# A two-batch conformer block on one core: the second batch's first query group is scored by quads, LayerNorm statistics beside attention move to ACT

## The chip, the cores and the metric

The kernel runs on one core of one Trainium2 chip. The metric is the device time of one execution in microseconds (us); the median of three runs is given, and beside it the time of the one execution that was profiled. All tensors in memory are bf16.

## The reference

Two sequences of T = 4000 tokens with D = 512 channels go through one conformer block. F is 2048; every LayerNorm is without weights.

```python
h = _layernorm(x);  x1 = x + 0.5 * (_silu(h @ w_ff1_a) @ w_ff1_b)
h = _layernorm(x1); q, k, v = h @ w_q, h @ w_k, h @ w_v
p = _softmax(einsum('btd,bsd->bts', q, k) * D ** -0.5)
x2 = x1 + einsum('bts,bsd->btd', p, v) @ w_o
h = _layernorm(x2) @ w_pw1
h = h[..., :D] * _sigmoid(h[..., D:])
dc = depthwise convolution of h over time, 3 taps per channel
dc = (dc - mean) / sqrt(var + 1e-5)      # per channel, over both sequences
x3 = x2 + _silu(dc) @ w_pw2
h = _layernorm(x3); x4 = x3 + 0.5 * (_silu(h @ w_ff2_a) @ w_ff2_b)
return _layernorm(x4)
```

## The kernel before

**Stages.** The tokens of a sequence are cut into seven chunks of 512 and one of 416, so there are 16 chunks for the two sequences. First the feed-forward block runs over all chunks, writes each chunk's residual to DRAM, and writes the normalised tokens ("keys") to DRAM as `keysd`. Then comes attention, with one query group per chunk: groups 0 to 7 are the first sequence, 8 to 15 the second. The convolution's first matmuls and taps of earlier groups run in the same slots. After attention come the end of the convolution and the second feed-forward block.

**Attention.** w_q and w_k are folded into one matrix M, w_v and w_o into another, so that keys and values are both the normalised tokens. A query group has 32 slots `kt`, one per tile of 128 keys; the last tile is a tail of 32. In a *plain* group each key tile is scored by four matmuls that stream 512 query columns. In a *quad* group tiles 0, 1 and 30 are scored plainly and the other 28 in seven quads of four tiles: `score_quad` makes a 2x2 product by seven products instead of eight (the form of Strassen and Winograd). Each of the seven is four matmuls of 256 columns. ACT copies the first and the fifth product, DVE adds them to others on the way (tiles `s`, `xt` in the trace, by their memories), and ACT takes the exponents. A quad needs three sums of key tiles (`k_sums`, stored to DRAM as `kfd`, fetched by `k_stream`), one difference that is put over a key tile, and sums of the queries (`q_sums`). In the kernel before, groups 0 and 8 are plain (`plain = g % TCB == 0`), and make the key sums of their sequence while they run. The product of the exponents with the values is by seven products in all groups; its sums on DVE are `pair_sums`, which also adds up the softmax's denominators. The second sequence's value sums are made ahead, in groups 1 to 5, by `v_ahead`: load, four DVE sums, stores.

**What happens around a group.** `keys_swap` replaces the first sequence's keys by the second's in groups 7 and 8: `key_queries` issues one DMA transpose for each of the 32 key tiles. `units_late` ends the group before: its last value products, `sums_by_query` (the denominators turned by DMA transposes and reduced by one DVE instruction), and `project` in slots 9 and 13, whose `residual` on DVE adds the attention to the tokens. Then `ln_job` makes LayerNorm's statistics (BATCH_NORM_STATS2 and BATCH_NORM_AGGREGATE on DVE, a power on POOL), and normalises on ACT. `tail_scores`, for the 32 last keys, comes in slot 21.

**Who sets the order.** The program is written down once as nodes with their reads and writes, and then `Plan` orders it for each engine by costs and due times (`n.late`): it is a list scheduler, with DMA on SP's queue. An engine executes its own list in order, with waits on semaphores. The costs that matter here are

```python
if e == "ACT":
    return 170 + 0.83 * n + (200 if isinstance(call.kw.get("scale"), bass.AP) else 0)
```

so an instruction on ACT has no extra cost for bringing out an accumulated sum. Every instruction of the kernel is issued by one helper, so all rows of the profile have the line L93, and tiles tell them apart.

Of the kernel before, what the change touches and what calls it, by code (L numbers as in the profile page):

```python
# [109 lines left out]
class Plan:  # L110
# [161 lines left out]
    def once(self):  # L272

        pe, T = self.pe, self.T
        for n in reversed(self.nodes):
            if n.e != "PE":
                n.late = min([s.late - self.lag(n, s) - (self.SPARE if n.size else 0) for s in n.succs] + [pe[min(n.at, len(pe) - 1)].late + 40000])
# [273 lines left out]
class Conformer:  # L551
# [35 lines left out]
    def memory(self):  # L587
# [119 lines left out]
        self.b_kfd = [[Buf("kfd") for _ in range(QUADS)] for _ in range(B)]  # L707
        self.vhd = nc.dram_tensor("vhd", [PAIRS, 128, 2 * D], BF16, kind="Internal").ap()
# [150 lines left out]

        self.hl = C.view(oHL, 1024).rearrange("p (h c k) -> p h c k", h=2, c=DC)  # L860
# [3 lines left out]
        self.b_sq = [Buf("sq") for _ in range(2)]  # L864
# [237 lines left out]

    def ln_job(self, c, kind, eng="DVE", plan=(1, 1, 2, 2, 3, 4, 5, 5, 6, 6), slot=None, pe=None):
# [122 lines left out]
    def residual(self, ps, b_ps, g, scalar, b_scalar=(), rows=slice(0, TILE)):  # L1226

        self.S.op("DVE", lambda e: e.scalar_tensor_tensor(
            out=self.XT[g][rows], in0=ps[rows], scalar=scalar, in1=self.XT[g][rows], op0=ALU.mult, op1=ALU.add),
            reads=[b_ps, self.bx[g]] + list(b_scalar), writes=[self.bx[g]])  # L1230
# [367 lines left out]
    def q_group(self, b, qc, dc):  # L1598
# [5 lines left out]
        for cc in range(DC):  # L1604
            self.mm(ps[:, 0:W], self.M[:, cc, dc * 128:(dc + 1) * 128], lin[:, cc, lo:lo + W],
                    cc == 0, cc == DC - 1, [self.b_M] + self.b_lnT[sl], b_ps)
        self.act(self.qT[s][:, dc, 0:W], ps[:, 0:W], AF.Copy, [b_ps], [self.b_qT[s][dc]])
# [148 lines left out]
    def pair_sums(self, g, j, step):  # L1756
# [20 lines left out]
        if step == 6:  # L1777
            S.op("DVE", lambda e: e.tensor_tensor(out=acc[:, 0], in0=acc[:, 0], in1=acc[:, 1], op=ALU.add),
                 reads=[self.b_acc[s]], writes=[self.b_acc[s]])
            return  # L1780
        sig = [ft[:, 0:2, at + k, 0:hw] for k in range(n)]
        if j == 0:
            S.op("DVE", lambda e: e.tensor_copy(acc, sig[0]), reads=b_f[0:2], writes=[self.b_acc[s]])
        elif j == GROUPS - 1:
            S.op("DVE", lambda e: e.tensor_tensor(out=acc, in0=acc, in1=sig[step - 4], op=ALU.add),
                 reads=b_f[0:2] + [self.b_acc[s]], writes=[self.b_acc[s]])
        else:
            two = self.P30[:, 0:W].rearrange("p (h k) -> p h k", h=2)
            out, x, y, rd, b_out = ((two, sig[0], sig[1], b_f[0:2], self.b_P30), (acc, acc, two, [self.b_P30, self.b_acc[s]], self.b_acc[s]))[step - 4]
            S.op("DVE", lambda e: e.tensor_tensor(out=out, in0=x, in1=y, op=ALU.add), reads=rd, writes=[b_out])  # L1790
# [115 lines left out]

    def v_back(self, j, which):
# [37 lines left out]
    def k_stream(self, g, q):  # L1945
        n, b = (QUADS * g + q) % 2, g // TCB
        self.load(self.KF[n].rearrange("p m u j k -> p (m u j k)"), self.kfd[b][q], self.b_KF[n], reads=[self.b_kfd[b][q]])
# [56 lines left out]
    ASIDE = {3: (5, 7), 4: (5, 7), 5: (5, 7), 6: (5, 7), 16: (0,), 20: (0,), 21: (1,)}  # L2004
# [35 lines left out]
    def forms(self, g, kt):  # L2040

        plain, more = g % TCB == 0, g + 1 < NCK and (g + 1) % TCB
# [11 lines left out]
        else:  # L2054
# [3 lines left out]
            if kt == 1 and g % TCB == 1:  # L2058
# [39 lines left out]
    def units_late(self, o, kt):  # L2098
# [5 lines left out]
        elif kt < 7:  # L2104
# [7 lines left out]
            if kt == 3 and o == NCK - 2:  # L2112
                self.sums_direct(o % TCB % 2)
        for ti in {9: (0, 1), 13: (2, 3)}.get(kt, ()):
            self.project(o, ti)
# [856 lines left out]
```

## Time and profile before

| | |
|---|---|
| median of 3 runs | 1879.53 us (1877.93 to 1880.09) |
| the profiled execution | 1879.47 us |
| its span, first to last instruction | 1875.6 us, mean granted TensorE clock 0.998 |
| busy: PE / DVE / ACT / POOL | 1857.5 / 1548.0 / 1278.0 / 124.2 us |
| DMA, mean over the span | 123 GB/s |

In the rows, PE is the matmul engine, PEld its weight loads, DVE the vector engine, ACT the scalar engine, POOL GpSimd, and SP the queue that issues the DMAs. A row names what is written and read as out<-in by the memories of the program: `s` and `y` are the PSUM banks, `keys` holds the key tiles, `xt` the residual tokens and the sums for the quads, `sums` the exponents and their sums, `work` the queries, transposed tokens and LayerNorm's small values, `wff` in attention the convolution's buffers and the staging for sums made ahead. The span's stages are feed-forward to about 403 us, attention from there to about 1400, the turn to the second feed-forward block until about 1450, and that block to the end. Group 8 lies at about 892 to 958 us.

### The profile page before, as it was taken

The numbers are of one execution on the slowest core, as the hardware profiler recorded it, in microseconds if no ns is written. First come the engines' busy times: TensorE is split into PE (matmuls) and PEld (weight loads), VectorE is DVE, ScalarE is ACT, GpSimd is POOL, SyncE is SP. The second block draws the span as 40 slices with busy tenths as digits, with TensorE's granted clock in tenths as the row PEclk, the third lists the DMA queues.
The fourth block names the chain that finished last, engine by engine and source line by source line (L and its number), as shares of the span: only waits on it lengthen the run. The fifth ranks groups of instructions, "written<-read, shape, count | busy, mean of one in ns | idle before, by whom it ended". The sixth has DMA issues, their size and how long they took to land.

```text
span 1875.6 us, 38994 instructions
## 1 busy us (share of the span) xinstructions
PE 1857.5 (99%) x15384; PEld 1445.4 (77%) x15384; DVE 1548.0 (83%) x3293; ACT 1278.0 (68%) x2190; POOL 124.2 (7%) x241
## 2 busy tenths in 40 slices
PE   9999999999999999999999999999999999999998
PEld 5888888866777777777677777777764888888886
DVE  7789989868778888877878788778878889889885
ACT  5777777754556666666557666666657787777774
POOL 1000000000000000000000001000011000000010
PEclk9999999999999999999999999999999999999999
DMA  7333344197545555448954444444365222221211
GB/s 197 86 89 91 80 112 107 53 275 208 172 142 159 155 171 160 117 130 175 254 123 133 134 119 114 126 138 122 107 205 158 66 69 69 72 54 48 63 33 56
DMA packets 325013, 231.51 MB, mean 123 GB/s; under 512 B 204179, under 2 KB 295638, under 8 KB 324566
## 3 DMA queue, kind: packets, MB, share of 16 engines
q1 hardware_dynamic: 324294, 228.68, 44.2%
q8 instruction: 123, 2.02, 0.4%
q14 instruction: 68, 0.56, 0.1%
q10 hardware_dynamic: 528, 0.26, 0.0%
HBM read 128.44 MB, written 55.79 MB: 98 GB/s over the span
## 4 chain that ended last, share of the span: by engine, by line
PE 97%; DVE 1%; ACT 1%; DMA 0%; issue 0%; SPq 0%; DVEq 0%; ACTq 0%
PE s L93 49%; PE y L93 49%; DVE work L93 1%; ACT work L93 0%; DVE wff L93 0%; DMA xt<-in_x_dram 0%; ACT sums L93 0%; DVE xt L93 0%; DVE s L93 0%; ACT xt L93 0%; ACT s L93 0%; DVE sums L93 0%; DVE keys L93 0%; ACT keys L93 0%; SPq L93 0%
## 5 line engine op out<-in xcount | busy, mean ns | idle before, releaser
L93 ACT ACTIVATE sums<-s 128x512 bf16<-128x512 f32 (+2 forms) x494 | 289.1, 587 | 234.3 <-PE s L93 232.8
L93 ACT ACTIVATE keys<-s 128x512 bf16<-128x512 f32 (+2 forms) x284 | 165.2, 587 | 141.4 <-PE s L93 115.8
L93 DVE TENSOR_TENSOR sums<-sums 128x512 bf16<-128x512 bf16 (+3 forms) x528 | 201.8, 399 | 63.5 <-ACT sums L93 53.1
L93 PE MATMUL y<-work,keys 128*128 128x256 bf16 x1920 | 244.8, 273 | 0.0
L93 PE MATMUL s<-work,keys 128*128 128x256 bf16 (+5 forms) x1456 | 225.1, 292 | 0.8 <-ACT sums L93 0.6
L93 PE MATMUL y<-wff,keys 128*128 128x256 bf16 (+3 forms) x1592 | 209.2, 276 | 0.1
L93 DVE BATCH_NORM_STATS2 work<-xt 128x6 f32<-128x512 bf16 x311 | 205.6, 683 | 3.9 <-DMA xt<-in_x_dram 3.3
L93 PEld LDWEIGHTS y<-work,keys 128*128 128x128 bf16 x1920 | 187.9, 98 | 25.1
L93 PE MATMUL y<-sums,keys 128*128 128x256 bf16 (+1 forms) x1440 | 204.8, 270 | 0.0
L93 PE MATMUL s<-sums 128*128 128x256 bf16 x1296 | 194.5, 273 | 0.0
L93 DVE TENSOR_TENSOR keys<-keys 128x1024 bf16<-128x1024 bf16 (+2 forms) x262 | 170.2, 663 | 26.2 <-ACT keys L93 20.8
L93 PE MATMUL y<-work,wff 128*128 128x256 bf16 (+2 forms) x1116 | 184.0, 292 | 0.0
L93 PEld LDWEIGHTS y<-wff,keys 128*128 128x128 bf16 (+1 forms) x1592 | 151.2, 98 | 32.4 <-issue 3.3
L93 ACT ACTIVATE work<-xt,work 128x512 bf16<-128x512 bf16 x208 | 160.1, 805 | 10.9 <-DVE work L93 9.1
L93 POOL TENSOR_TENSOR work<-work 128x4 f32<-128x4 f32 (+3 forms) x92 | 88.3, 963 | 1108.3 <-DVE work L93 1108.3
L93 PEld LDWEIGHTS y<-sums,keys 128*128 128x128 bf16 x1440 | 139.1, 98 | 22.7 <-issue 0.2
L93 PEld LDWEIGHTS s<-work,keys 128*128 128x128 bf16 (+1 forms) x1456 | 119.3, 97 | 48.2 <-issue 4.7
L93 PEld LDWEIGHTS s<-sums 128*128 128x128 bf16 x1296 | 126.7, 98 | 20.0
L93 PE MATMUL s<-work,wff 128*128 128x512 bf16 (+5 forms) x668 | 140.5, 345 | 1.4 <-ACT work L93 1.1
L93 PE MATMUL y<-sums,xt 128*128 128x256 bf16 (+1 forms) x960 | 141.2, 270 | 0.3 <-DVE sums L93 0.3
L93 PE MATMUL s<-work 128*128 128x512 bf16 (+4 forms) x565 | 137.5, 373 | 2.4 <-DVE work L93 1.7
L93 PEld LDWEIGHTS y<-work,wff 128*128 128x128 bf16 x1116 | 108.2, 98 | 29.7
(140 smaller groups left out, 3195.8 us busy)
## 6 DMA issues: line engine op xcount, KB each, us to landing
xt<-kfd SPq DMA_DIRECT2D x98, 384.0 KB, 3.2
xt<-v12d SPq DMA_DIRECT2D x105, 256.0 KB, 3.0
xd<-xt SPq DMA_DIRECT2D x28, 512.0 KB, 3.0
xt<-xd SPq DMA_DIRECT2D x28, 512.0 KB, 3.8
out_dram<-xt SPq DMA_DIRECT2D x14, 512.0 KB, 2.9
xt<-in_x_dram SPq DMA_DIRECT2D x13, 512.0 KB, 4.1
dcvd<-wff SPq DMA_DIRECT2D x48, 128.0 KB, 2.7
keys<-dcvd SPq DMA_DIRECT2D x12, 512.0 KB, 4.0
```

The source lines that it names most:

```text
L93: return getattr(eng, self.name)(*self.args, **self.kw)
```

## The change

1. Group 8 scores by quads (`plain = g == 0`). The second sequence's key sums are made in groups 1 to 6 by `k_ahead`, in turn with `v_ahead`, which moves from a period of 10 slots to one of 6 for both: two DMA transposes of key tiles into a staging tile, four DVE sums, a store of the tiles to the new `khd`, and two stores to `kfd`. `k_back` brings the tiles back by a plain load of two tiles; only tiles 0, 1, 30 and the tail are still transposed in groups 7 and 8.
2. LayerNorm beside attention (`ln_beside`): the residual's DVE instruction also gives each token's sum, POOL scales it to a negative mean, ACT squares the centred tokens with an accumulated sum, and POOL does the rest. This takes the place of 4 statistics and 4 aggregates on DVE per group.
3. The denominators are reduced by four ACT copies with an accumulated sum per group, in place of one DVE reduction.
4. `pair_sums` adds the first two and the last pairs in bf16 before they go to the f32 sum.
5. `tail_scores` moves to slot 9 from group 1 on, always in bank 1; `touch` adds a matmul of 96 columns behind a 416-wide query projection that lands in bank 1.
6. In `Plan`, no instruction outside PE is due more than 8000 ns before PE's place in the program where it was written.

In whole numbers of instructions, from the built programs: PE has 112 fewer matmuls of 512 columns, 196 more of 256 and 4 more of 96; DVE has 119 instructions fewer, ACT 130 more, POOL 60 more, and SP issues 56 DMAs more.

```diff
-                n.late = min([s.late - ... for s in n.succs] + [pe[...].late + 40000])
+                n.late = max(pe[min(n.at, len(pe) - 1)].late - 8000, min([s.late - ... for s in n.succs] + [pe[...].late + 40000]))
...
+    def touch(self, ps, b_ps, W):
+        if W < CHUNK and b_ps is self.bank(1)[1]:
+            x = self.hT[0][:, 0, 0, :]
+            self.mm(ps[:, W:CHUNK], x, x[:, 0:CHUNK - W], False, True, [self.b_hT[0][0]], b_ps, skip_group_check=True)
...
+    def ln_spread(self, c, sl, ti):
+        x, b_x = self.tokens(c, ti)
+        self.act(self.ltm[ti][0:TILE, :], x, AF.Square, [b_x, self.b_mv[sl][ti]], [self.b_ltm[ti], self.b_st[sl][ti]],
+                 bias=self.mv[sl][:, ti, 0:1], accum_out=self.st[sl][:, ti, 1:2])
...
-        if j == 0:
-            S.op("DVE", lambda e: e.tensor_copy(acc, sig[0]), reads=b_f[0:2], writes=[self.b_acc[s]])
-        elif j == GROUPS - 1:
-            S.op("DVE", lambda e: e.tensor_tensor(out=acc, in0=acc, in1=sig[step - 4], op=ALU.add),
-                 reads=b_f[0:2] + [self.b_acc[s]], writes=[self.b_acc[s]])
+        t, b_t = (self.P30, self.b_P30) if j < GROUPS - 1 else (self.last7, self.b_last7)
+        if step == 4:
+            out, x, y, rd, wr = two, sig[0], sig[1], b_f[0:2], [b_t]
+        elif j == 1:
+            out, x, y, rd, wr = acc, two, f0[:, 0:2, 1, 0:hw], [b_t] + b_0[0:2], [self.b_acc[s]]
...
+    def k_ahead(self, i, step):
+        S, (q, u) = self.S, divmod(i, 2)
+        if step == 0:
+            for r in range(2):
+                src, rd = self.key_source(1, self.quad_tiles(q)[2 * u + r])
+                self.transpose(self.vst[:, r * D:(r + 1) * D].rearrange("p (c k) -> p c k", c=DC), src, rd, b_x)
+            return
+        if step < 5:
+            ...
+            S.op("DVE", lambda e: e.tensor_tensor(out=out, in0=x, in1=y, op=op), reads=rd + b_x, writes=wr)
+            return
+        self.store(self.khd[i], self.vst, b_x, [self.b_khd[i]])
+        self.store(form[:, 0:2, u], ..., b_2, [self.b_kfd2[q][2 * u]])
+        self.store(form[:, 2, u], self.vs1, b_1, [self.b_kfd2[q][2 * u + 1]])
+
+    def k_back(self, i):
+        self.load(self.hq[:, q, u].rearrange("p r e j k -> p (r e j k)"), self.khd[i], b, reads=[self.b_khd[i]])
...
-            W, plain = width(g), g % TCB == 0
+            W, plain = width(g), g == 0
...
+                if kt == (9 if g else 21):
+                    self.tail_scores(g)
...
-                if kt == 21:
-                    self.tail_scores(g)
...
+            if ti % 2:
+                self.ln_middle(self.ln_conv, slice(ti - 1, ti + 1))
...
-        i, r = divmod(at - KT - 4, 10)
-        if 0 <= i < PAIRS:
-            for n in {0: (0,), 4: (1, 2), 5: (3, 4), 8: (5,)}.get(r, ()):
-                self.v_ahead(i, n)
+        i, r = divmod(at - KT - 4, 6)
+        for n in {0: (0,), 2: (1, 2), 3: (3, 4), 5: (5,)}[r] if r in (0, 2, 3, 5) else ():
+            if i % 2 == 0 and 0 <= i // 2 < PAIRS:
+                self.v_ahead(i // 2, n)
+            elif i % 2 and 0 <= i // 2 < 2 * QUADS:
+                self.k_ahead(i // 2, n)
...
-                    self.key_queries(1, k)
+                    if k < 2 or k > KT - 3:
+                        self.key_queries(1, k)
+                    elif k % 2:
+                        self.k_back((k - 2) // 2)
...
-            S.op("DVE", lambda e: e.tensor_reduce(
-                self.sq[s], self.sT[0:TILE].rearrange("p h c k -> p c h k"), AX.XY, ALU.add),
-                reads=self.b_sT, writes=[self.b_sq[s]])
+            for ti in range(TPC if not self.any_score else 0):
+                x = self.sT[0:TILE, :, ti]
+                self.act(x, x, AF.Copy, self.b_sT, [self.b_sqs[s][ti]], accum_out=self.sq[s][:, ti:ti + 1])
...
-                self.ln_job(g - 1, "in", "ACT", (1, 2, 5, 6, 7, 8, 8, 9, 10, 11), slot=0)
+                self.ln_beside(g - 1, self.ln_conv, (2, 3, 6, 7, 7, 8, 9, 10, 11))
```

More of the change, by code (lines that the diff above doesn't have):

```diff
@@ L1946, in k_stream @@
         n, b = (QUADS * g + q) % 2, g // TCB
[L1947 removed]
+        self.load(self.KF[n].rearrange("p m u j k -> p (m u j k)"), self.kfd[b][q], self.b_KF[n],
+                  reads=self.b_kfd2[q] if b else [self.b_kfd[b][q]])
     def score_quad(self, g, q, step):
@@ L2040, in forms @@
     def forms(self, g, kt):
-        plain, more = g % TCB == 0, g + 1 < NCK and (g + 1) % TCB
+        plain, more = g == 0, g + 1 < NCK
         if more and 27 <= kt < 31:
```

85 lines of the change are left out of this document (67 added, 18 removed).

## The prediction, made before the changed kernel was run

> **What bounds the kernel now.** I read the page first (busy shares and the chain), then busy time by stage, then PE's own waits in those stages, then ACT's and PE's single rows. The page:
>
> ```profile
> PE 1857.5 (99%) x15384; PEld 1445.4 (77%) x15384; DVE 1548.0 (83%) x3293; ACT 1278.0 (68%) x2190; POOL 124.2 (7%) x241
> ...
> PE 97%; DVE 1%; ACT 1%; DMA 0%; issue 0%; SPq 0%; DVEq 0%; ACTq 0%
> ```
>
> The chain that ended last is PE for 97% of the span, at a mean granted clock of 0.998. Time comes out only where PE has fewer columns to stream or waits less. The table by stage has a window, its length, then busy us and counts of PE, PEld, DVE, ACT, POOL, then clock, DMA share, GB/s. The windows are query group 8 (the second batch's first, plain before), steady quad group 10, and group 15 (416 queries):
>
> ```profile
> 892.00:958.00 66.00, 65.14 (x455) 39.92 (x453) 52.03 (x126) 35.68 (x61) 2.94 (x11) 1.00 0.84 224
> 1020.00:1083.00 63.00, 63.00 (x517) 47.70 (x515) 48.41 (x102) 38.31 (x68) 2.78 (x7) 1.00 0.44 122
> 1334.00:1387.00 53.00, 51.05 (x498) 41.93 (x496) 42.24 (x98) 35.53 (x69) 2.73 (x9) 1.00 0.52 162
> ```
>
> A steady quad group keeps PE busy without a hole while DVE works 48 and ACT 38 of 63 us. Group 8 is longer, has holes, and has the highest DMA share of the three (0.84). PE's waits (who waited for whom: us, times, longest), for 835 to 958 us and then for 1334 to 1403 us:
>
> ```profile
> PE s L93 <- ACT sums L93: 0.6, 1, 0.6
> PE s L93 <- DVE s L93: 0.4, 1, 0.4
> PE s L93 <- DVE sums L93: 0.3, 1, 0.3
> PE s L93 <- DVE xt L93: 0.2, 1, 0.2
> ```
>
> ```profile
> PE s L93 <- ACT sums L93: 0.7, 2, 0.6
> PE s L93 <- DVE s L93: 0.4, 1, 0.4
> PE s L93 <- DVE xt L93: 0.4, 1, 0.4
> PE y L93 <- DVE sums L93: 0.3, 1, 0.3
> ```
>
> The same view for 958 to 1334 us, groups 9 to 14, is empty. For group 1 (460 to 521) it has 0.6 us in two waits. So the query groups hold 1.5 + 1.8 + 0.6 = 3.9 us of PE idle in 11 waits. What PE does per matmul comes from its timeline (start, length, count), once for 512 columns and once for 256:
>
> ```profile
> 26.25 2.75 PE L93 MATMUL s<-work,wff 128*128 128x512 bf16 x12
> 28.84 0.60 PE L93 MATMUL y<-work,keys 128*128 128x256 bf16 x4
> ...
> 489.20 0.60 PE L93 MATMUL y<-sums,xt 128*128 128x256 bf16 x4
> 489.63 0.60 PE L93 MATMUL s<-xt 128*128 128x256 bf16 x4
> 490.07 0.60 PE L93 MATMUL s<-work,keys 128*128 128x256 bf16 x4
> 490.51 0.60 PE L93 MATMUL y<-sums,xt 128*128 128x256 bf16 x4
> ```
>
> Start to start, 512 columns cost 2.59/12 = 0.216 us and 256 columns (490.51 - 489.20)/12 = 0.109 us. A 256-wide record lasts 0.273 us, so its shown end runs 0.164 us into its successor: each wait costs about 0.16 us more than its shown idle. The 11 waits cost 3.9 + 1.8 = 5.7 us.
>
> **The change, part by part.**
>
> *Quads in group 8.* 28 key tiles of 4 matmuls of 512 columns go: 112 x 0.216 = 24.2 us. Seven quads of 7 products of 4 matmuls of 256 come: 196 x 0.109 = 21.4 us. That is **-2.8 us** on the path. The rows bear this out directly, because groups 9 to 14 run this same mix without a hole. [...]
>
> *Four filler matmuls (touch)* of 96 columns after the 416-wide query projections: rows have 56 ns for 128 columns and 98 ns for a weight load, so 0.2 to 0.4 us; I take **+0.2**, nearest to the matmul row.
>
> *Group 8's own waits* (0.6 + 0.3 us in 892 to 958, with the overlap 1.2 us) sit in the plain scoring's exponents. In the quad form that follows, the view is empty. **-1.2 us**; bounds 0 and -1.2.
>
> *Work taken from DVE.* Per group it loses 4 statistics (0.686), 4 aggregates (0.185), one reduction over the transposed sums (1.215), the shift (0.165), a copy (0.42), and trades one f32 add (0.685) for a bf16 one (0.42): 5.5 of about 48 us. The tail scores leave slot 21, about where groups 1, 7 and 15 wait, for slot 9. The remaining waits there cost 5.7 - 1.2 = 4.5 us; seven of the nine were ended by DVE. Bounds 0 and -4.5; I take half, **-2.2 us**, as ACT ended the other two and gets more work.
>
> *Work given to ACT.* Per group 4 squares of 512 (0.60) and 4 copies of 256 (between 0.29 at 128 and 0.60 at 512, taken as 0.39), each with an accumulator read:
>
> ```profile
> 35.99 1.23 ACT L93 ACTIVATE work<-s 128x512 bf16<-128x512 f32 x2 [1.14 <-PE s L93]
> 37.11 0.19 ACT L93 ACTIVATION_READ_ACCUMULATOR work<-s 128x1 f32 x1
> 37.20 0.59 ACT L93 ACTIVATE keys<-s 128x512 bf16<-128x512 f32 x1
> ```
>
> That is 4 x 0.79 + 4 x 0.58 = 5.5 us shown, on 38 to 42 of 63. It lies beside PE, but ACT's queue is in order: behind a square stand exponents and the copy of the first product, for which PE's next product waits. The planner's cost for an activation (170 + 0.83n) has no term for the read, and the read puts off the next start by 0.09 us, so ACT runs late against its order by 8 x 0.09 = 0.74 us per group if nothing absorbs it. What absorbs it (ACT's groups in 958 to 1335 us; last field: idle before, and who ended it):
>
> ```profile
> L93 ACT ACTIVATE sums<-s 128x512 bf16<-128x512 f32 x136 | 80.9, 595 | 80.2 <-PE s L93 79.5
> ...
> L93 ACT ACTIVATE xt<-s 128x512 f32<-128x512 f32 x42 | 25.1, 597 | 25.6 <-PE s L93 25.3
> ```
>
> ACT sits idle 0.6 us on average before an exponent and before the first product's copy, so nearly all is absorbed. Bounds 0 and 15 x 0.74 = +11.1 us; I take **+1.0**, near the covered end. Without that cover it would be the whole 11.1. DVE's four residual sums per group also bring out an accumulator; no row has that on DVE, and with ACT's read (0.09) as a stand-in it is 0.4 us per group against 5.5 taken off: nothing.
>
> *Key sums ahead.* Groups 1 to 6 get 14 sets: two transposes, four DVE sums (0.28 each), three stores. Group 8 loses 28 sums of 0.42, its own 7 stores and 28 of the transposes in this row:
>
> ```profile
> L93 SPq DMA_TRANSPOSE keys<-keysd x30: 1188/1202/1863, 835.5 to 929.1; - x30
> ```
>
> SP's queue takes 28 x 1.2 + 42 x 0.45 = 53 us more over some 370 us; behind them stand the streams of key and value sums, issued about five slots (10 us) before use, that land in 3.2 us, so nothing waits. The DMA share there (0.55) has room; group 8's 0.84 falls, and its 14 plain loads (5.2 to 5.4 us for 256 to 512 KB in the loads of values) are issued 5 to 24 slots (10 us or more) ahead. A wait is added: the first sum waits for transposes (3.5 us to land) at the head of DVE's queue, with pair sums and the adds that PE needs behind it. DVE waited like this for transposes up to 0.9 us in groups 1, 2 and 11, and PE's only waits in these groups come 28 us later. I price it at 0, bounds 0 and 14 x 0.9 = +12.6 us.
>
> *New order elsewhere.* The limit on due times (8000 ns) moves ACT and DVE instructions in the feed-forward stages too, though PE's first 3,604 matmuls keep their order. No PE wait shows between 50 and 400 or 1450 and 1850 us. The tail between (1403 to 1450) has chained waits that can fall either way: 0, within 1.5.
>
> Sum: -2.8 + 0.2 - 1.2 - 2.2 + 1.0 = **-5.0 us**. The profiled execution took 1879.47 us (span 1875.6 and 3.9 around it), the median is 1879.53, so the forecast is **1874.5 us**.
>
> **Rivals.** 0.2% is 3.8 us, about what a measurement of this kernel can tell from no change.
> - *All waits of the query groups go*, DVE being what ended most: -2.8 + 0.2 - 5.7 = -8.3, 1871.2. For: DVE ended seven of those nine. Against: group 15 packs the same instructions into 53 us.
> - *Only the columns count*: the waits come back as others, as ACT takes up what DVE gives: -2.6, 1876.9. For: three of the eleven waits are ACT's already.
> - *ACT becomes late (the slower side)*: the reads and 5.5 us more per group delay the first product's copy. All 0.74 us exposed in 15 groups gives -6.0 + 11.1 = +5.1, 1884.6. It is slower by 3.8 us from 9.8 us, 0.65 per group, on. Against: 0.6 us idle before that copy.
> - *Late transposes hold DVE*, all 14 exposed: -5.0 + 12.6, 1887.
> - *Weight loads show*: if the 84 extra loads (98 ns) did not hide behind 256-wide matmuls, +8.2 - 2.8 and the other terms (-2.2) make +3.2, 1882.7, within 0.2%. The 0.109 us row, with one load to each matmul, excludes it. [...]
>
> **How the numbers follow.** Forecast 0.46; all waits go 0.16; columns only 0.23; ACT late 0.10; transposes 0.04; weight loads 0.01. Faster by over 0.2% is the first two, 0.62; same is columns only and the weight loads, 0.24; slower the other two, 0.14. Range 1869.5 to 1882: the low end is all waits and 1.5 from the tail; the high end reaches into the late cases and leaves some 0.1 beyond.
>
> **What would show it.** Right: 112 fewer matmuls of 512 columns and 196 more of 256; group 8 some 4 us shorter with an empty PE wait view; transposes gone from 835 to 930 us; fewer waits in groups 1, 7, 15. Wrong: PE waits on ACT in groups 9 to 14, where there are none now, DVE waits on wff<-keysd transposes followed by PE holes, or a new hole in the feed-forward stages.

## The result, and the profile after

After takes 1895.71 us in the median (1893.55 to 1898.54, 4 runs), before 1879.07 beside it (1877.93 to 1880.09, 4 runs): a ratio of 1.0087, 95% interval 1.0071 to 1.0103. The change costs 16.6 us where 5 us of gain were forecast. The profiled execution of after took 1898.54 us, its span is 1894.0, 18.4 us longer than before's. First the page's busy line and chain:

```profile
PE 1865.9 (99%) x15472; PEld 1451.1 (77%) x15472; DVE 1471.5 (78%) x3234; ACT 1316.3 (69%) x2436; POOL 132.9 (7%) x301
...
PE 87%; DMA 5%; DVE 4%; ACT 3%; issue 1%; SPq 0%; POOL 0%; DVEq 0%; ACTq 0%
```

PE is still 99% busy, but the chain that ended last is PE for 87% only, where before it was 97%. DMA, which was 0% of the chain, is 5%, and DVE 4%. DVE's own work fell by 76 us (1548.0 to 1471.5) and ACT's rose by 38, as the change says: more room on DVE, and a later end.

Where the time went can be read from one kind of PE's rows, the last value product of each group (`y<-wff,keys 32*128`), which comes early in the next group. Its first start in each group marks the same place in every kernel. Before has it at 460.95 us for group 0, at 892.80 for group 7, at 958.28 for group 8 and at 1387.32 for group 15; after at 460.74, 906.13, 970.08 and 1403.22. So groups 1 to 7 are 13.5 us longer, group 8 is 1.5 us shorter, groups 9 to 15 are 4.1 us longer, and what lies around them 2.3. The loss sits where the key sums are made ahead, not where ACT alone has more work.

Group 8 and the steady group 10, in windows that follow these marks (length, then busy us and counts of PE, PEld, DVE, ACT and POOL, clock, DMA share, GB/s):

```profile
906.00:970.00 64.00, 62.41 (x535) 46.94 (x532) 45.22 (x103) 44.94 (x89) 3.81 (x15) 1.00 0.83 220
1034.10:1097.10 63.00, 63.00 (x514) 47.40 (x514) 43.29 (x96) 42.79 (x86) 3.27 (x11) 1.00 0.43 121
```

Group 10 is as long as it was and PE has no hole in it, with DVE down from 48.4 to 43.3 us and ACT up from 38.3 to 42.8. Group 8 has the 455 matmuls of before turned into 535, and holes of 1.6 us. PE's waits (the lines of 0.8 us or more in all), first for groups 1 to 6 (460 to 849), then for groups 7 and 8 (849 to 970):

```profile
PE s L93 <- DVE s L93: 3.7, 6, 2.1
PE s L93 <- DVE xt L93: 2.1, 4, 1.0
PE s L93 <- ACT s L93: 0.8, 1, 0.8
```

```profile
PE s L93 <- ACT s L93: 1.7, 2, 1.3
PE s L93 <- DVE s L93: 1.0, 3, 0.4
```

In groups 1 to 6, where before had 0.6 us in two waits (460 to 835), PE waits 6.6 us on the first three lines, and DVE is what it waits for nearly always. What DVE and ACT themselves wait for over the whole span is new:

```profile
DVE sums L93 <- DMA work<-work: 15.3, 15, 4.2
DVE wff L93 <- DMA wff<-keysd: 13.1, 13, 2.6
ACT work L93 <- DMA work<-work: 9.5, 9, 2.7
```

Before, DVE's line for `wff<-keysd` was 0.5 us in one wait, its line for `sums` behind `work<-work` 5.6 in eleven, and ACT had none. The three lines belong to different stages. The thirteen waits on `wff<-keysd` all lie in groups 1 to 6: ten (10.4 us) end with a transpose for the key sums, three (2.7 us) with a load for the value sums, which go through the same staging tile. ACT's nine waits lie in attention too, behind the transposes that turn the softmax's denominators; before, DVE stood 2.2 us in three waits for these. DVE's fifteen waits of `sums` on `work<-work` lie outside attention, before 308 us and after 1467 us, in the two feed-forward blocks. SP, which issues all these DMAs, stands too, since all sums ahead go through one staging tile:

```profile
SPq L93 <- DMA wff<-keysd: 13.6, 11, 2.5
SPq L93 <- DMA vhd<-wff: 13.1, 10, 3.4
SPq L93 <- DMA khd<-wff: 7.6, 5, 2.3
```

Here `vhd<-wff` is a store that must land before the next set may be staged (6.9 us in 4 waits before). The transposes that were added for the key sums (time to issue one, ns: least, median, most; then first and last start in us):

```profile
L93 SPq DMA_TRANSPOSE wff<-keysd x28: 1188/1190/1578, 469.6 to 800.7; - x28
```

They land 2.7 us after issue in the median, the slowest of the 28 after 5.0. One chain from such a transpose to PE, from the timeline (start, length, what, idle before it and who ended that):

```profile
740.65 1.19 SPq L93 DMA_TRANSPOSE wff<-keysd  x1
...
743.11 0.62 DVE L93 TENSOR_TENSOR wff<-wff 128x256 bf16<-128x256 bf16 x2 [1.30 <-DMA wff<-keysd]
...
744.04 0.68 DVE L93 TENSOR_TENSOR xt<-s,xt 128x512 f32<-128x512 f32 x1
...
744.78 0.61 PE L93 MATMUL s<-xt,keys 128*128 128x256 bf16 x4 [0.98 <-DVE xt L93]
```

The transpose is issued at 740.65. DVE's first key sums (`wff<-wff`, two of them) are already at the head of DVE's queue and stand 1.30 us for it. Behind them is `xt<-s,xt`, an addition to a product that PE's next product needs, so PE idles 0.98 us. The largest of these:

```profile
768.98 1.19 SPq L93 DMA_TRANSPOSE wff<-keysd  x1
...
773.42 0.29 DVE L93 TENSOR_TENSOR wff<-wff 128x256 bf16<-128x256 bf16 x1 [2.59 <-DMA wff<-keysd]
773.63 0.69 DVE L93 TENSOR_TENSOR s<-s,xt 128x512 f32<-128x512 f32 x1
...
774.38 1.03 PE L93 MATMUL s<-xt,keys 128*128 128x256 bf16 x4 [2.06 <-DVE s L93]
```

DVE stands 2.59 us and PE idles 2.06. This is the sign of being wrong that the prediction named: DVE waits on `wff<-keysd` transposes followed by holes of PE. Its other signs came small: one PE wait on ACT in groups 9 to 14 (0.24 us), and three new holes in the second feed-forward block (0.49 us at 1486, 0.30 at 1494, 0.41 at 1814).

### The profile page after: what moved, and what is told of

Same layout as the page of the kernel before. It is cut to its first block, busy times and chain, and to the rows that moved or that the text cites. A ratio compares the mean times of both kernels' runs of the same rounds, so it can differ in the third digit from the quotient of the medians.

```text
span 1894.0 us, 39494 instructions
## 1 busy us (share of the span) xinstructions
PE 1865.9 (99%) x15472; PEld 1451.1 (77%) x15472; DVE 1471.5 (78%) x3234; ACT 1316.3 (69%) x2436; POOL 132.9 (7%) x301
## 4 chain that ended last, share of the span: by engine, by line
PE 87%; DMA 5%; DVE 4%; ACT 3%; issue 1%; SPq 0%; POOL 0%; DVEq 0%; ACTq 0%
PE y L93 44%; PE s L93 43%; DMA wff<-keysd 2%; DVE work L93 1%; ACT work L93 1%; DMA work<-work 1%; DMA vhd<-wff 1%; DVE s L93 1%; DVE xt L93 1%; DVE wff L93 1%; DVE sums L93 1%; ACT sums L93 0%; ACT wff L93 0%; ACT keys L93 0%; ACT xt L93 0%
## 5 line engine op out<-in xcount | busy, mean ns | idle before, releaser
L93 ACT ACTIVATE sums<-s 128x512 bf16<-128x512 f32 (+2 forms) x487 | 284.5, 585 | 165.1 <-PE s L93 164.1
L93 DVE TENSOR_TENSOR sums<-sums 128x512 bf16<-128x512 bf16 (+3 forms) x528 | 192.4, 398 | 56.2 <-ACT sums L93 52.5
L93 ACT ACTIVATE work<-xt,work 128x512 bf16<-128x512 bf16 x268 | 207.5, 787 | 13.2 <-DVE work L93 9.6
L93 PE MATMUL s<-work,keys 128*128 128x256 bf16 (+5 forms) x1400 | 205.0, 284 | 0.9 <-DVE xt L93 0.8
L93 PE MATMUL y<-work,wff 128*128 128x256 bf16 (+2 forms) x1132 | 187.8, 293 | 0.3 <-ACT keys L93 0.3
L93 DVE TENSOR_TENSOR keys<-keys 128x1024 bf16<-128x1024 bf16 (+2 forms) x255 | 166.1, 669 | 20.7 <-ACT keys L93 14.4
L93 DVE BATCH_NORM_STATS2 work<-xt 128x6 f32<-128x512 bf16 x251 | 164.1, 680 | 3.7 <-DMA xt<-in_x_dram 3.0
L93 PEld LDWEIGHTS s<-work,keys 128*128 128x128 bf16 (+1 forms) x1400 | 113.1, 97 | 45.0 <-issue 4.3
L93 PE MATMUL s<-xt,keys 128*128 128x256 bf16 (+1 forms) x872 | 133.2, 271 | 8.8 <-DVE s L93 6.7
```

Source lines behind the costliest of these rows:

```text
L93: return getattr(eng, self.name)(*self.args, **self.kw)
```

## The experiments

Three theories stood at the start. **T1**: the key sums ahead hold DVE's queue and SP's in groups 1 to 7, because their transposes land later than the order allows for. **T2**: ACT's added work (squares, copies, accumulator reads) makes ACT late. **T3**: the limit on due times (part 6) spoils the order everywhere. All runs in one table: the median, the ratio to before (an estimate of its own, not the quotient of the medians), and how much longer than before the stages of the one profiled execution are, by the marks above (us).

| run | what it is | median us | over before | ratio, 95% interval | groups 1-7 | group 8 | 9-15 | around |
|---|---|---|---|---|---|---|---|---|
| after | the change | 1895.71 | +16.6 | 1.0087, 1.0071-1.0103 | +13.5 | -1.5 | +4.1 | +2.3 |
| e1_companion | after, group 8 plain, no key sums ahead | 1887.98 | +8.3 | 1.0040, 1.0026-1.0054 | +5.8 | -0.1 | +2.5 | 0 |
| e2_quads | before with quads in group 8 alone | 1906.67 | +27.0 | 1.0140, 1.0123-1.0157 | +16.8 | +3.0 | +1.2 | +5.2 |
| e3_landing | after, transposes planned 1.5 us later | 1884.62 | +4.9 | 1.0026, 1.0016-1.0036 | +5.0 | -1.1 | +2.1 | -1.9 |
| e4_nowait | after, key sums don't wait for transposes | 1891.55 | +11.8 | 1.0058, 1.0042-1.0075 | +12.5 | -1.1 | +1.9 | +1.1 |
| e5_nosums | after without the key sums ahead | 1884.76 | +4.8 | 1.0025, 1.0016-1.0034 | +3.8 | -1.2 | +1.9 | +0.6 |
| e6_before_landing | before, transposes planned later | 1879.25 | -0.7 | 0.9994, 0.9985-1.0003 | +0.4 | -0.4 | +0.4 | +0.2 |
| e7_noclamp | e3 without the limit on due times | 1888.35 | +8.4 | 1.0042, 1.0028-1.0055 | +7.3 | -1.1 | +2.1 | +0.3 |
| e8_dvesums | e3, denominators on DVE | 1885.91 | +6.0 | 1.0032, 1.0019-1.0044 | +5.5 | -0.6 | +2.2 | -1.4 |
| e9_companion_landing | e1, transposes planned later | 1885.29 | +5.1 | 1.0026, 1.0015-1.0037 | +4.9 | -0.6 | +2.4 | -0.5 |
| e10_quads_planned | e2 with limit and later landing | 1882.06 | +1.8 | 1.0010, 1.0001-1.0019 | +1.7 | -1.2 | +1.2 | -0.8 |
| e11_tailback | e3, part 5's tail undone | 1880.39 | +0.2 | 1.0001, 0.9992-1.0010 | +3.4 | -0.7 | +0.3 | -0.4 |
| e12_acccost | e3, accumulator reads in the costs | 1885.79 | +5.6 | 1.0031, 1.0019-1.0042 | +7.0 | -1.7 | +2.4 | -0.3 |
| e13_tail_only | after, part 5's tail undone | 1898.10 | +17.9 | 1.0102, 1.0087-1.0117 | +15.7 | -1.5 | +0.5 | +2.0 |
| e14_tail_dvesums | e11, denominators on DVE | 1882.10 | +1.9 | 1.0010, 1.0001-1.0019 | +1.7 | +1.0 | +0.5 | -1.6 |
| e15_tail_land4 | e11, planned 3 us later | 1887.07 | +6.9 | 1.0037, 1.0024-1.0051 | +6.5 | -0.6 | +2.1 | -1.0 |
| e16_quads_land4 | e10, planned 3 us later | 1890.69 | +10.5 | 1.0060, 1.0048-1.0072 | +8.6 | +2.1 | +1.3 | -1.4 |
| e17_quads_limit | e2 with the limit | 1890.20 | +10.5 | 1.0045, 1.0031-1.0059 | +8.6 | +2.0 | +0.3 | +0.5 |
| e18_quads_pairs | e10 with part 4 | 1885.31 | +5.6 | 1.0026, 1.0017-1.0035 | +3.3 | +2.6 | +0.8 | +0.6 |

The median of before beside them lay between 1879.1 and 1880.2 us; how far a run is from before is taken from the before of its own comparison.

**Halves of the change.** `e1_companion` keeps parts 2 to 6 and leaves group 8 plain; `e2_quads` puts part 1 with its `touch` on before.

```diff
 e1 (against after)
-            W, plain = width(g), g == 0
+            W, plain = width(g), g % TCB == 0
-        i, r = divmod(at - KT - 4, 6)
+        i, r = divmod(at - KT - 4, 10)
...
-            elif i % 2 and 0 <= i // 2 < 2 * QUADS:
-                self.k_ahead(i // 2, n)
 e2 (against before): the lines of part 1 and touch, nothing of parts 2 to 6 else
```

> The changed kernel without its quads in group 8: no key sums ahead, no plain transfers back, group 8 plain, value sums ahead at the old period of 10 slots; the LayerNorm on ACT, the denominators on ACT, the early tail scores and the due-time limit stay. Theory 1 (the key sums ahead hold DVE and SP's queue in groups 1 to 7, where the changed kernel lost 13.6 us): groups 1 to 7 come back to within 3 us of the kernel before, and the whole lies at 1880 to 1887 us. Theory 2 (the work given to ACT, with its unplanned accumulator reads, is what delays PE): groups 1 to 7 keep most of the loss, 1888 us or more. Theory 3 (the new due times spoil the order everywhere): the same as theory 2 in time, but with waits also outside attention.

> The kernel before with only the quads in group 8: key sums ahead in groups 1 to 6, plain transfers back, value sums ahead at the period of 6 slots; LayerNorm and denominators stay on DVE, tail scores in slot 21, no due-time limit. Theory 1: groups 1 to 7 lose some 10 us or more, DVE waits for transposes of wff<-keysd as in the changed kernel, and the whole is at 1886 us or more. Theories 2 and 3: groups 1 to 7 as before, group 8 some 3 us shorter, 1875 to 1878 us.

The two halves cost 8.3 and 27.0 us, 35 together, where the whole costs 16.6: they are not terms that add up. `e1_companion` lies between what T1 and T2 expected, in time and in groups 1 to 7. Quads without the companion are the worst kernel of all. In its profile DVE stands 15.0 us for `wff<-keysd`, and 15.9 for `work<-work`, 6.7 of them in attention. Of its 5.2 us around the groups, 4.8 come ahead of the first mark, with one hole of PE that ends at 459.87, where group 1 begins. So T1's place is right, and the companion or the limit must take something off it.

**The lateness of the transposes.** Three edits of after, each aimed at one link of the chain from SP to PE.

```diff
 e3 (against after; Plan.once)
-                n.land = pipe - s + 1000
+                n.land = pipe - s + (2500 if n.turn else 1000)
 e4 (against after; k_ahead): the sums read the folded matrix M, which is long there, not the staged tiles
-        a11, a12, a21, a22 = [self.vst[:, n * HD:(n + 1) * HD] for n in range(4)]
+        a11, a12, a21, a22 = [self.M[:, n // 2, n % 2 * HD:(n % 2 + 1) * HD] for n in range(4)]
...
 e5 (against after); group 8 scores with other data of the same size
-            elif i % 2 and 0 <= i // 2 < 2 * QUADS:
-                self.k_ahead(i // 2, n)
-        self.load(self.hq[...], self.khd[i], b, reads=[self.b_khd[i]])
+        self.load(self.hq[...], self.vhd[i], b, reads=[self.b_vhd[i]])
...
-        self.load(self.KF[n]..., self.kfd[b][q], ...)
+        self.load(self.KF[n]..., self.kfd[0][q], ...)
```

> The changed kernel with one number changed in the planner: a transposing DMA is taken to land 1.5 us later than it was (1000 becomes 2500 ns behind the modelled pipe), so that what uses it is put later into the engines' orders. Theory 1, as far as it is DVE and ACT standing at the head of their queues before the transposes have landed: DVE's waits for wff<-keysd fall from 13.1 us to under 5 and ACT's for work<-work from 9.5 to under 4, and the whole falls by 5 to 12 us, to 1884 to 1891. Theory 2: no more than 2 us less.

> The changed kernel, with the second sequence's key sums made from another tile that always lies ready (so these sums are not the reference's) and not put over the staging tile: the same transposes, the same number of DVE sums and the same stores, but DVE does not wait for the transposes. If it is DVE's wait for the transposes that costs: 8 us or more less, 1888 us or less, PE's waits on DVE in groups 1 to 7 mostly gone. If it is SP's queue, held by the one staging tile whose stores must land before the next load, that makes everything behind it late: under 4 us less.

> After without the key sums made ahead: no transposes, sums or stores of k_ahead in groups 1 to 6; group 8 keeps its quads and its plain transfers, but fetches other data of the same size, so its scores are not the reference's. T1 (the key sums ahead hold DVE and SP's queue): groups 1 to 7 lose 7 to 10 of the 13.5 us they gained over before, 1885 to 1889 us; what is left is the companion's 6. T2 (ACT's added work behind transposes is the cost everywhere) and T3 (the due-time limit spoils the order): within 3 us of after, 1893 or more.

Leaving the key sums out gives back 11.8 of the 16.6 us (`e5_nosums`). Keeping every one of them, and only telling the planner that a transpose lands 1.5 us later, gives back 11.7 (`e3_landing`): the instructions, the bytes and the DMAs are those of after, only their order differs. So these us are not the price of the work or of DMA bandwidth. They are the price of an order that was planned for earlier landings. The line holds for every transpose, though, the denominators' and the feed-forward blocks' too, and no run moves the key sums' alone. In `e3_landing` the two lines of DVE's waits are

```profile
DVE wff L93 <- DMA wff<-keysd: 1.9, 3, 1.4
DVE sums L93 <- DMA work<-work: 1.5, 2, 0.8
```

against 13.1 and 15.3, and ACT's line is gone. The profiled execution is 14.4 us shorter than after's: 8.5 in groups 1 to 7 (5.0 instead of 13.5), 2.0 in groups 9 to 15, 4.2 around the groups, and group 8 is 0.4 longer. Some of this is PE's clock, which was granted at half for 3.41 us in before (at 1407.84), for three such stretches in after (at 774.37, and two in a row at 1443.38) and for none in `e3_landing`; a stretch costs up to an estimated 1.7 us, half of its 3.41 (1.66 for the one at 774.37, see the last section).

`e4_nowait` lies between its two forecasts: with the sums' own wait for their transposes taken away, 4.8 us come back. But groups 1 to 7 are only 1.0 us shorter than in after. DVE stands there still, 9.4 us in seven waits for values loaded to `wff`, and PE's two largest holes (1.98 us until 583.44, 2.91 until 634.07) follow two of these waits, of 2.10 and 3.05 us. So it is not the sums' own wait alone: what passes through SP's queue and the single staging tile comes late for the values too. That the queue and the tile are the reason is argued from this, not shown by a run. Nor is it told apart whether the later landing helps because transposes land later than planned, or because it leaves room for what SP issues late: the transpose issued at 740.65 landed after 2.4 us, 0.3 later than the planner has it, and DVE stood 1.30.

The waits alone are a poor measure of the price. In `e5_nosums` ACT stands 16.0 us, in ten waits, for the denominators' transposes, and the kernel is 11 us faster than after, where that line is 9.5. Most of ACT's standing is covered; DVE's, with the additions behind it that PE needs, is not.

**Is it the change's, and is it the limit?** A control on before, and the limit taken out of `e3_landing`:

```diff
 e6 (against before): the line of e3
 e7 (against e3)
-                n.late = max(pe[...].late - 8000, min([...] + [pe[...].late + 40000]))
+                n.late = min([...] + [pe[...].late + 40000])
```

> Before, with the planner told that a transposing DMA lands 1.5 us later. T1: before has few transposes that an engine stands behind, so this gives 0 to -2 us, 1877.5 to 1880. Rival (the planner's landing time is a fault of the kernel before as well, and the -11 us it gave in after were not the change's cost): 1870 to 1876, and after with the same planner would still be 10 us or more behind it.

> After with the later landing, and without the limit of 8000 ns on due times. T3 (the limit spoils the order): 1876 to 1880. T1 and T2: 1882 to 1888, as with the limit; more than that if the limit is what lets DMAs leave early enough.

Before doesn't profit: 0.9994, and its interval takes in 1. In attention it has few DMAs of this kind that an engine stands behind (2.7 us), as T1 says. And without the limit `e3_landing` gets 3.5 us slower, so T3 is wrong here: the limit helps. How much it does for the quads was told apart later:

```diff
 e17 (against e2): with the limit on due times, landing as it was
 e10 (against e17): the line of e3
```

> Before with the quads of group 8 and the key sums ahead alone, with the limit on due times and the planner's landing as it was. It parts the 24.6 us that the limit and the later landing gave together on the quads alone. If the landing did it: 1896 to 1907, with DVE's waits for wff<-keysd and work<-work at 10 us or more each. If the limit did it: 1882 to 1888.

> Before with the quads of group 8 and the key sums ahead alone, with the limit on due times and the later landing, and with none of the companion (parts 2 to 5). T1 (the cost is the lateness of transposes that the order does not know of): most of the +27 us that the quads alone cost goes, 1880 to 1886. Rival (DVE is too full for 56 sums more without the companion's relief): 1890 or more, with PE waits on DVE in groups 1 to 6 and no DMA waits behind them.

By the medians, of the 27.0 us of the quads alone the limit takes 16.5, and the later landing 8.6 of what is left. (`e17_quads_limit` fell between its two ranges; its five runs go from 1886.60 to 1890.85, and by its ratio it is 8.5 us behind before, not 10.5.) At 1882.06 us the quads are then 1.8 us slower than before, and DVE's wait for `wff<-keysd` is 5.7 us instead of 15.0. The landing was expected to be the larger part; the limit is. The rival, that DVE is too full for these sums without the companion's relief, falls: `e10_quads_planned` has none of it.

**What the companion costs.** Beside the transposes, `e3_landing`, `e5_nosums` and `e9_companion_landing` all end 4.8 to 5.1 us behind before; what they share, and `e10_quads_planned` lacks, is the companion.

```diff
 e9 (against e1): the line of e3
 e8 (against e3; sums_by_query): one DVE tensor_reduce again, no ACT copies
 e12 (against e3; Plan.cost)
-            return 170 + 0.83 * n + ...
+            return 170 + 0.83 * n + (92 if 'accum_out' in call.kw else 0) + ...
-        return 150 + rate * n
+        return 150 + rate * n + (80 if 'accum_out' in call.kw else 0)
 e11 (against e3): tail_scores in slot 21, its bank from sbank(), ASIDE with 21: (1,) as before; touch kept
```

> After without the quads of group 8 and the key sums ahead (the companion alone: parts 2 to 6), with the later landing. If the companion's +8.3 us is ACT and DVE standing behind the turned denominators, the later landing takes most of it: 1878 to 1882, waits of ACT for work<-work transposes from 17 us to under 2. If it is ACT's added work itself (T2), 1885 to 1888 as without.

> After with the later landing, and with the denominators reduced by one DVE instruction as before, not by four ACT copies. T2 (ACT's copies behind the turned denominators hold ACT's queue): 1877 to 1881. T1 (the later landing has already moved the copies behind their transposes): 1883 to 1886, since DVE takes 1.2 us per group again and ACT gives 2.3.

> After with the later landing, and with 92 ns for ACT's and 80 ns for DVE's accumulator reads in the planner's costs. If ACT's lateness against its order is what is left (the third of the prediction's slower cases): 1879 to 1882. If not: 1884 to 1886.

> After with the later landing, and the tail scores back in slot 21 and in whichever bank is next, as before (part 5 undone, touch kept). If the tail's place is what costs 1 us each at ACT's copy of the fifth product in groups 6, 8, 14 and 15: 1880 to 1882. If those waits come from ACT's added squares and copies: 1884 to 1886.

`e9_companion_landing` missed the range for the transposes and lies in that for T2. ACT's waits for the denominators went from 16.9 us to 0.5 as expected, and the time only from +8.3 to +5.1 us: those waits were worth some 3 us. (Its end so near `e3_landing` is in part chance: 3.1 of its us are in group 7, where PE waits 2.20 us for a `work<-work` DMA.) Giving the denominators back to DVE brings nothing (+6.0 against +4.9), and neither does a price for the accumulator reads (+5.6). LayerNorm's squares stay on ACT in all these runs, and none takes them away by themselves. But `e11_tailback` keeps all of ACT's added work and is even with before, at 1880.39 us, so T2 does not explain what was left. Its gain is where part 5 had left a mark: groups 6, 14 and 15 are 0.1, 0.0 and 0.2 us longer than before instead of 2.6, 1.2 and 0.9. (The profiled execution shows 1.5 us of gain against `e3_landing` in all, the medians some 4.5: it is the slowest of its eleven runs, and groups 1 to 3 and the stages around are 1.5 us longer each, these with a stretch of half clock at 1410.32 that `e3_landing` lacks: the mean granted clock is 0.998 against 1.000.) In the eight kernels of the table that have part 5, after aside, group 14 is 1.2 us longer than before, group 6 by 1.2 or more and group 15 by 0.7 to 0.9; in the ten that don't have it groups 14 and 15 are longer by 0.3 at most. In `e3_landing` the wait in group 14 is at 1321.62: PE idles 0.85 us for ACT's copy of the fifth product (`s<-s`, 1320.97 to 1321.57), which has two exponents and the copy of the next group's 416-wide queries (`work<-s 128x416`, 1319.05) ahead of it. `e11_tailback` has no PE wait between 1290 and 1345 us. Whether the slot, the bank or the place of those queries does it was not told apart.

**What is left.** Two orders of undoing, two later landings still, and the version that the runs pointed to:

```diff
 e13 (against after): the edit of e11 alone
 e14 (against e11): the edit of e8
 e15 (against e11), e16 (against e10)
-                n.land = pipe - s + (2500 if n.turn else 1000)
+                n.land = pipe - s + (4000 if n.turn else 1000)
 e18 (against e10): pair_sums of part 4
```

> After with the tail scores back in slot 21 and in whichever bank is next, and the planner as it was. If the tail's place and the late transposes are two separate costs, the -4.2 us that this gave on top of the later landing comes here too: 1890 to 1893, with the waits for transposes as in after. If they are one and the same (a later tail leaves ACT the room to wait in), more: 1882 to 1888.

> After with the later landing, the tail scores back, and the denominators reduced on DVE as before. What is left of the companion is then LayerNorm's squares and the bf16 adds. If ACT's copies still cost something in groups 1 to 3 (+3.3 us there): 1876 to 1879. If not: 1880 to 1882.

> After with the tail scores back and transposes planned to land 3 us later than in after (instead of 1.5), which covers the slowest of the key sums' transposes. If what is left in groups 1 to 3 is still lateness of transposes: 1877 to 1879.5. If it is work that has no room: 1880 to 1882.

> Before with the quads of group 8 and the key sums ahead alone, the limit on due times, and transposes planned to land 3 us later. With 1.5 us DVE still stood 5.8 us behind the key sums' transposes and groups 1 to 3 were 1.8 us longer. If that is the rest of the cost, what is left is the gain in columns: 1877 to 1880. If not: 1881 to 1883.

> The version that the experiments point to: before with the quads of group 8, the limit and the later landing, and of the companion only the part that takes work from DVE and gives none to ACT (the bf16 adds of part 4). If DVE's 0.7 us per group of relief ends the waits of groups 1 to 3 (1.8 us) : 1878 to 1880.5, below before only if group 8's -2.7 us of columns then comes through. If the order falls otherwise: 1881 to 1884.

`e13_tail_only` fits neither expectation. With the transposes planned as in after, undoing part 5 costs 1.3 us instead of giving 4.8, though groups 14 and 15 lose their mark here too (the intervals of the two kernels overlap): in groups 1 to 7 DVE stands 16.3 us for `wff<-keysd`, and PE has five holes of 1.3 to 2.1 us. While the order rests on landings that don't come true, where its holes fall is chance of a few us, and a single edit can't be priced in it.

`e14_tail_dvesums` is no gain either (+1.9): with the denominators back on DVE groups 1 to 3 are 2.0 us shorter than in `e11_tailback`, and group 8 is 1.7 longer.

Landings planned at 3 us later, which is past the slowest of after's 28 (5.0 us), make both kernels worse again by 6.7 and 8.7 us, outside both ranges that were expected. DVE's waits on `wff<-keysd` stay low (3.3 and 5.3 us), and PE waits for additions on DVE, up to 1.2 us at a time, in places where it did not; in `e16_quads_land4` a wait of 3.63 us for ACT's copy in group 8 comes on top. So "later" is not "safer": the best of the three landings tried is the middle one, and it is not shown to be the best there is.

`e18_quads_pairs` missed: 1885.31 where 1878 to 1880.5 or 1881 to 1884 was expected. Groups 1 to 7 are worse by 1.6 us against `e10_quads_planned`, and group 8 by 3.8. For group 8 the timeline shows why:

```profile
926.45 1.08 POOL L93 TENSOR_TENSOR work<-work 128x4 f32<-128x4 f32 x1 [17.39 <-DVE work L93]
...
927.85 1.52 ACT L93 ACTIVATE work<-xt,work 128x512 bf16<-128x512 bf16 x2 [4.73 <-DVE work L93]
...
929.88 0.58 ACT L93 ACTIVATE s<-s 128x512 f32<-128x512 f32 x1
...
930.51 0.33 PEld L93 LDWEIGHTS s<-xt 128*128 128x128 bf16 x4 [3.77 <-ACT s L93]
```

ACT's normalisation of group 7's tokens (`work<-xt,work`) is at the head of ACT's queue and stands 4.73 us for LayerNorm's chain, which has only now reached the power on POOL. Behind it are the copies of the first and the fifth product, and PE idles 3.49 us until `s<-s` is done. A wait on this copy near the middle of group 8 is in nearly every kernel that scores the group by quads: 1.30 us in after, 0.87 in `e3_landing`, 1.30 in `e11_tailback`, 1.36 in `e10_quads_planned`, 2.42 in `e14_tail_dvesums`, 3.63 in `e16_quads_land4`, 3.41 in `e17_quads_limit`, 4.20 in `e2_quads`. A plain group has no such copy. Why this chain is later in group 8 than in groups 9 to 14 stays open.

No version beats before: the two that come level are `e11_tailback` (1880.39) and before itself with the later landing.

## Why the prediction was wrong

**The step that failed is "Key sums ahead", priced at 0.** Its reasons were that the streams behind the 53 us on SP's queue are issued 10 us before use, "so nothing waits", and that DVE's waits for transposes had covers. Both were read from a trace in which hardly anything waits for the staging tile (0.5 us, once). The streams did hold: few waits name `kfd` or `v12d`. The other users of the queue did not. With the key sums on it, and a staging tile that has to be emptied by stores before the next set goes in, the key sums' transposes and the loads of values came after DVE was ready for them. (The denominators' are another matter: ACT stands longer for them without the key sums, 16.0 us in `e5_nosums`.) The upper bound of the step, 12.6 us, is close to what was measured: 11.8 by `e5_nosums`, with DVE standing 10.4 us in ten waits for transposes, and 2.7 in three for values, where the bound had 14 waits. The bound was about right, and the value and the chance (0.04 for this rival) were not. The order's plan was the thing to look at: it lands a transpose of 128 KB 2.1 us after its issue when the queue is empty (400 ns, the bytes at 180 per ns, and 1000 ns), and the row of before showed 2.5 us at the least and 3.5 in the median for such transposes; the prediction read the 3.5, and did not set it beside the plan.

**The cover was misjudged.** The prediction noted that additions PE needs stand behind the sums and counted PE's waits in groups 1, 2 and 11 as evidence of cover. It didn't ask what happens when thirteen such waits fall in six groups, some of them just ahead of an addition that PE needs. The row at 744.78 us answers: 1.30 us of DVE became 0.98 of PE.

**The columns were right**, and the only term that came as predicted: PE's time in group 8 without its waits, each matmul taken at the median step of its width (0.216 us for 512 columns, 0.109 for 256), falls from 63.4 to 60.7 us, -2.7 against -2.8. The group's length shows 1.5 of it.

**Group 8's own waits, -1.2, was wrong.** "In the quad form that follows, the view is empty" was read from groups 9 to 14. Group 8's own waits, the overlap in them, are 1.8 us where before had 1.2. The largest is ACT's copy of the fifth product (1.30 us at 938), the wait that `e18_quads_pairs` shows large.

**DVE's relief, -2.2, did not come.** DVE's busy time fell by the 5 us per group that were counted, 48.4 to 43.3, but the waits of groups 1, 7 and 15 went from 1.0, 1.0 and 2.7 us (with the overlap) to 1.2, 2.4 and 3.7. A DVE with more room was waited for as before; what stood ahead in its queue is the likelier reason.

**ACT, +1.0: the cover held, and the tail scores were missed.** ACT's idle time before an exponent and before the first product's copy, in the six quad groups 9 to 14, is now

```profile
L93 ACT ACTIVATE sums<-s 128x512 bf16<-128x512 f32 x136 | 80.8, 594 | 56.4 <-PE s L93 56.1
...
L93 ACT ACTIVATE xt<-s 128x512 f32<-128x512 f32 x42 | 25.1, 599 | 31.8 <-PE s L93 31.8
```

so 0.41 us before an exponent, from 0.59, and 0.76 from 0.61 before the copy: the cover held, and a price for the reads changes nothing (`e12_acccost`). What ACT's copies are exposed to is the tail scores' place. The prediction named it only as a relief, under the work taken from DVE, and had no cost for it; by `e11_tailback` part 5 costs some 4.8 us once the landing is mended.

**New order elsewhere.** The stages around the query groups took 2.3 us more in after and less than before in most planned kernels. The bound of 1.5 was too small, and up to 1.7 us of the 2.3 is one stretch more of half clock than before had.

So of the 16.6 us, 11.7 come back when the order is planned for later transposes, and 4.8 more, once that is mended, when part 5 is undone. They hold for this order of undoing: part 5 undone first gave nothing (`e13_tail_only`). With both mended the rest of the change comes to +0.2: the -2.7 of columns are in it, eaten by group 8's new wait and by waits in groups 1 to 3 (+3.3 us in `e11_tailback`).

## What to carry to other kernels

Price work that is made ahead by when its transfers land: ask what stands behind its first instruction in the engine's queue, and compare the planned landing (2.1 us for the transposes here) with the landing column of the trace (2.7 us in the median, 5.0 at the most) before pricing it at zero. Telling the planner was worth as much as leaving the work out (11.7 and 11.8 us), and a landing planned too late cost most of it again (6.7 and 8.7 us). And free an engine for what it delays: 76 us off DVE bought nothing that shows in these runs, where PE's waits on DVE followed what stood ahead in its queue.

## What the runs showed of the hardware

One of PE's holes cost more than its length. Behind the 2.06 us in the timeline above, PE's granted clock is 0.50, and 0.99 again from 777.77 on, in windows after it (PE's busy time is the second field, the clock the third from the end):

```profile
776.07:777.75 1.68, 1.68 (x5) 0.58 (x4) 1.24 (x5) 1.12 (x2) 0.00 (x0) 0.50 0.48 103
777.77:778.20 0.43, 0.43 (x5) 0.39 (x4) 0.11 (x1) 0.22 (x1) 0.00 (x0) 0.99 0.73 207
```

Four matmuls of 512 columns took 1.70 us instead of 0.86, and eight of 256 before them 1.69 instead of 0.87. The half clock lasted 3.41 us, from 774.37 on, so this hole cost 2.06 + 1.66 us. The length of a hole alone did not decide here. The mean clock over the 3.4 us behind a hole was 0.50 after this one of 2.06 us, 0.53 after 4.20 (`e2_quads`, from 949.4 on), 0.56 after 3.49 (`e18_quads_pairs`, 930.5), 0.61 after 3.41 (`e17_quads_limit`, 935.6), 0.67 after 2.84 (`e2_quads`, 459.9), 0.68 after 1.98 (`e4_nowait`, 583.5), 0.69 after 3.63 (`e16_quads_land4`, 935.4), and 1.00 after 2.91 (`e4_nowait`, 634.1).

In before and after, the half clocks begin whole multiples of 3.413 us apart, the length of one stretch. In after they begin at 774.37 and 1443.38 us, 669.01 or 196 times 3.413 apart; in before at 1407.84 and, behind PE's last matmul, at 1872.06, 464.21 or 136 times 3.413 apart. With windows laid on these starts, PE's idle time in the window ahead of a half clock is 1.89 us in before (1404.43 to 1407.84, in holes of 0.97 and 0.91) and 2.04 and 2.09 in after (770.95 to 774.37 and 1439.97 to 1443.38). The second of the two in a row, at 1446.79, follows a window at half clock with 1.01 us. In the other windows of the two traces, from 10 to 1860 us, PE idles 1.33 us at the most in before and 1.16 in after, and the clock of the next is 1.00. The hole of 2.91 us in `e4_nowait` lies in two windows, neither of which has more than 1.56 us of idle (3.41 less 2.06 and less 1.85), and the clock stays at 1.00:

```profile
629.10:632.51 3.41, 2.06 (x19) 1.59 (x17) 0.92 (x3) 3.41 (x6) 0.00 (x0) 1.00 0.88 278
632.51:635.92 3.41, 1.85 (x13) 1.29 (x14) 2.06 (x5) 0.44 (x2) 0.00 (x0) 1.00 1.39 180
635.92:639.33 3.41, 3.41 (x34) 2.86 (x32) 1.62 (x5) 2.87 (x6) 0.00 (x0) 1.00 0.95 159
```

From what idle time on the clock is halved, and whether that decides alone, these few windows don't show.

In after, each accumulated sum on DVE in groups 9 to 14 comes out by an instruction of its own, as ACT's do: 24 times DVE_READ_ACCUMULATOR, 83 ns, against ACT's ACTIVATION_READ_ACCUMULATOR, 48 times, 187 to 190 ns.
